# Linear branch's logits beside both value products of a segment, a narrower mask product, a new order of operations

## Chip, core and metric

The kernel runs on one core of one Trainium2 chip. The metric is device time in microseconds (us) of one launch, as the median of several runs. TensorE multiplies matrices into PSUM, which has 8 banks of 128 partitions by 512 fp32 columns; ScalarE and VectorE read PSUM; GpSimd works in SBUF alone. The profile calls the engines PE, ACT, DVE and POOL, and the loading of matmul weights PEld.

## What is computed

Two attention branches over the same 2048 tokens of width 512 are mixed by a gate for each token.

```python
# branch A: a recurrent memory of M=8 tokens, segments of 32 tokens, 32 heads of 128
mask = (idx[:, None] < M) | (idx[:, None] >= idx[None, :])
for s in range(64):
    h = concat([mem, x[32*s : 32*s+32]])            # 40 tokens
    q, k, v = h @ Wq, h @ Wk, h @ Wv                # per head
    p = softmax(where(mask, q @ k.T * 128**-0.5, -1e9))
    o = (p @ v) @ Wo
    mem = o[:8]; outs.append(o[8:])
# branch B: 32 heads of 16, 4 segments of 512 tokens, causal softmax inside a segment,
# plus a linear memory M, z of the segments before, mixed by a gate per head
    p = softmax(q @ k.T * 16**-0.5 + causal_mask)
    a_dot = p @ v
    a_mem = (phi(q) @ M) / (phi(q) @ z + 1e-6)
    o = g * a_mem + (1 - g) * a_dot;  M += phi(k).T @ v;  z += sum(phi(k))
out = gate * a + (1 - gate) * (b @ wo)
```

## The kernel before

**Branch A sets the pace.** Segment s needs the eight memory rows that segment s-1 gives, so 64 segments follow one another. `p_seg` issues one segment. It projects 32 rows, as many as a column group has columns (8 memory rows and 24 tokens), with weights streamed as 128x512 matmuls in four column groups (line 1399), copies PSUM to SBUF (line 999, on ScalarE or VectorE), and transposes q and k by head on VectorE (line 1464). The 32 heads are handled in two halves, r = 0 and 1, of 16 heads. The eight last tokens of each segment are projected four segments at a time (`p_rest`); they are called the rest here, and their queries, keys and values stand in `rem_q`, `rem_k`, `rem_v`.

For each half there are: a mask product H (line 1472) that writes the whole score bank with zeros and large negative numbers, from `neg` and `hide`; the scores S (lines 1479 and 1483) added onto it; an exponential into `PT` (line 1487); the sums over keys by a product U with a block matrix of ones (line 1502); a logarithm and an exponential on ScalarE that give the reciprocals `rc` (lines 1506 and 1508); two multiplications of `PT` by `rc` (line 1510 on VectorE, line 1513 on VectorE or GpSimd); the value product PV (lines 1544 and 1549), whose four row groups write four banks, a *quad*; and two copies of the quad to `OT` (line 999). Behind both halves come the output projection (line 1298, 64 matmuls), a copy `par`, a product `fold` (line 1022, fp32, 16 matmuls) that adds two column groups, and a copy to the next segment's memory rows (line 1321). `PT` holds for each half 224 columns: first 160 (4 heads of 40 queries) against the keys of the 32 rows, then 64 (4 heads of 16 queries) against the keys of the rest. The mask product covers all 224 columns.

**Branch B fills.** It has 16 units (4 segments by 4 groups of 8 heads) of two halves q. A half has four pieces, each of 320 columns of logits: `p_logits` (bL, line 1139, 4 or 8 matmuls in four row groups, into four banks), then `p_exps`: two exponentials of 128x640 on ScalarE (line 1157), a causal mask on GpSimd (line 1163) and, behind the fourth piece, the product with the values (line 1180). From unit 3 on `plan` places these pieces among the segments. `quad` gives each half the segments at which it begins and ends: 17 halves have two segments and 9 have three. A piece in `carry` is issued inside a segment: its logits use columns 160 to 480 of the four banks in which the value product of r=1 writes columns 0 to 160. A piece in `alone` takes four banks of its own. By `plan` 61 pieces are carried and 43 are alone; the 24 pieces of units 0 to 2 are alone as well.

**Tile modes.** TensorE runs three arrangements here: `c32` (four column groups of 32, all large products), `r32` (four row groups of 32 or 16: bL and PV) and `full`. Some products are FLEX: they take `c32` or `full`, whichever the neighbour before has.

**What sets the order.** Each engine runs its list in order. The lists are not found at build time: `ORDER` is a packed string of positions in the list of all operations, engine by engine, in TensorE, ScalarE, VectorE, GpSimd, SyncE order. `sequences` unpacks it; `schedule` then assigns banks along this order, and `waits` derives semaphore waits from the data and bank dependencies. Two engines that read the same PSUM banks are kept apart: the second waits for the first.

Of the kernel before, what the change touches and what calls it, by code (L numbers as in the profile page):

```python
# [8 lines left out]
ALU = mybir.AluOpType  # L9
# [6 lines left out]
    "c-nPZ2S5|&+kf6%lFK3qLs4;|f`D6aQ>!9cC$?gtPPAA@t<+t`g(4MKwQg-4t+wdjja6JI?g1+9i56E~pb!#5a_@cbU6RXP@Ix}Vd+wRPXT9wRxdE(TE7QZ&WVFaSec^ly"  # L16
    "W0(U;D`4TH*ZW(weG>Aa#pLw&KXpC!y~?{dy}d0aZNZOAUtd1a<wTo)(=rQ_mdnh_@jv;t3*XRd$FJ7cS#WkO1e@{#3#w@2nT2&9FI`mtN?1Ki0~6=Z8Ld7VeKZ=D#BSHb"
    "T#3jC+5oE?M4xN_<)rCpuT>VHSzSg?3k@0HK;%g(0svHLbIw9|c4t_1z>KgQmPVYOb}Tot?Xb2@sY?^jM6R{T!)}9bl{>Zng}P7bC}nzp^Fh9W=f1pUq^>vjE2qIya=k3Z"
    "VggW`9~w?B+Yh04PK;Uy5uJ!U;C~K5Yo9}{FAY`L5Jh>}?O?eK5ys+cZDnvKQhlULy#p;=q%go|-Jc_Ut&D=HVzsCuk9tu>DljkGjO#v!!de9u2w4{^Fg^f%vhY|dQrHaS"
    "8Zv*ZE-zNy*H;J4?K;Y<Z|b%(gUUg97|LS~1H>w93fteK+MhF%YX(c(3y6HGLvQ3<o+mI(0{CUJEt8=cq5=@Y*R?GMo1J<Djc*2?gU?Sv%@E>o$4|Ar(8eD?juZ?-bkJ2O"  # L20
    "Z04dsdx=W^^nbAp@71pjuLRQq0G7pmb6Q7PX>IYxDsO7ZA44sQDkrYf!Lk_(U`ocnse&5$08MHgjAkf`Suz*QUO-vOG-ZTR{WM?zK$c)yry0=o7;L)C5Uyz9OqCoys?El7"
    "vu=J`+5CC`+nQs6=o|;>jSis~^G9xoVGi^|UKUk}+`9-gcFInHQkG5b|FuovN|c4d9yh(M423?dSpbFL1Kxpf1;TFv3cW+TX3s!_1wZUbj9>LVz)^%~E7B?|6d%=3gYWyj"
    "tz}-@zmW+R!Hfkba|G(I^IGnx-;z*M$Yub!o%-POUaqK6eXRD%D}5#{c<lNFIALl{RH$LnzVNNM6{!EHrpwE`O1#vm0fV*yj27Hg2jIzzxIzu0d|y{BFV!<<_|G3yO1oLD"
    "-UuxrH#}?&z<7amdT?;)U(JRRoKaeUGVm_anrM&#Y#M9-ZKA+7WsYIpL|#pc%Az)F<#Uo$KLeze0w`(09tD6^so^j{(=x`QD+L0WUnVV?Rkj3va+_22P<ZYa-bAFKRCgq>"
    "iRD3cE@_?x!@ZXF>%nl&=QBZW`pR)D3k}nM<9NQS2djFITj}fbUfnbwm4a4l3cDTlFb!a~z<MIA8?~f+qb$xIZ!0Kl@?s-;-{pjQPxsDnYs;YR3!e(SFOpX){kHEA`O$I!"
    "Hx|=C5<yd@bnEIvUT<U0>KWQ*_^417RC@&>6{WzrDDsTD<)zls63C;fpa&fB+^_+2_HjsEGm~TtL8-A=C7TC3ADKWI4DeDAy)g{hjc5ZY2vLj|m?v&1@h0glE7f&6scwC)"
    "{Z<%qMbKaz#J7)`GJ>$xTC6Pq9t1rsBLz$OmZZzr)g)T4_4`H=9Y+4alg9)6^WjkWcs>n$E6hC(sp*?Fp!=!MVM8++iI+cQLn}}NDRuzIAO}+RT-(R_t4EGSh00*XctZu)"
    "snp~h!)BzUK&lYkQ6#)8yb^ZuN-HYNdRrOE8=XzQaBkw-mmA%L*C~6moAy2=V-$3$j^rU2?G=`YoAQPPoXfvor3Uy;FfRz;esIEOt;uM~=&Rj6$m_X}YBgNlSf-QP>?F_s"
    "`nF8D|J4-Yy7a0113T|Gj%n6^8wr|Msg6W#=g49LHrXaf(5y;O-Xs*w1?E?t#-4=)im}lhZre?CIVhXmkd+#OZ)-Aohdz2uC~62=KLn_+yB5uPf+E!%R2IXJ=?uw)w%6?~"
    "x!Yx+PFn7&361}$Mc$RwCrwh==vMh)DUZCox1V8i>Wzid7EVu_PC%4#d$|zsOIwDu9@AwChYb?%-(ZBAE>fE{9M~GeJ$D8X*3U9WTND-rNuhFDUaI11?r4BN2d@PYEH6M?"  # L30
    "Q**{ZmD-S=tBIHEk%DDL8Y1>R?EO)Y>pgYpn<@k-jKZs!(#bz+NXT>#0?n@)Xg<p>e*ojo2`qmCNc-!?KdA0=#;cfC$xDa_v{XjSuCFy)2Tn~{1~5xdbJ9E5y#44=J_bwX"
    "m`U~$q$ALp#5x}Ckq^BIRyadS6e_yHqy?M&@R#<U<mM59S8e#UZ*9<US;+ZaSE{0I_QydbuYw*l%?~?7DEbJre*?s2C}&s@rLd@!x#8tE8yoTf8p7RB(Aq6<4*GFnIz>n$"
    "Ir=~-Ftt=5E2?t3^(AO?vAQ?u{v>y7q?xNpsZ`!<Oqezo_@DY<fR6eD@uYYo1-V+TT0dG|thH0CVT{`T%T92orBCn7_oO)JXe-g>?@{II)uRfks~?3HubEpyZr^LN=OH9J"
    "8BbdXQ#X9GdThrWhs!8V3!1Lr(DkUX{f-@=1xI?e14lg>dUiT_5H^!`jtE#<!6i~0NcuF+hT3JiQW8)9z=AReE8uz89FjJ@?=VOGHj`3s<g($P-kdk8f~$>@#Jd~vf?_Dz"
    "riBkmzTLsg0F}%{$^mg0Pjm(%k8aOlx@GeT5P2bG-g`Bq&ME<a6Db(i_RcL3U^RFYKzrlCc#`6zbjm-1nx2qeqBiRw@Kv>Eq%puuQGy2@3<B(!40u@4#G_|BlFqr)-8hlq"
    "&qN0|z7P}jWbmkoz5EeC8$oPsfTv&Py>Jz54t1Yh=3qycH-9O#Y`$dsJ?YHBEYne7ffK4>wkCjP<>>NFVYjCWJO=`7+qd(WOSaBV7lDezMP27nebVh+R(S0=$<?1D3Jb-J"
    "3?zPr3VVyI9HD)4lE96Og&(NB!_o4|q@jQC1(3ZnT7gV9{&I`T#S5A0IK{oLs*_tNJ3r3YY07z@=8Y)i3Jg?v^QO@)XmqQkm-VBb8&q_qIx<L~gC2*Xj{CHeJ0CegUR0e!"
    "5b_e6u)H%y-;l%!yF%&)<RoBp_qnC{EExV8qjfk4ieUGT7<K9a6=!lWin@YPWb<obx#17MM*Gs(0Qj@_*zY=YEXl{wV7US9?}V-%55&(kb|jK1Q>O;YsXkz*Wq5=SY+XM="
    "!5GP<1@JT2$_)szY5Xk#uTfo2E5U9dSF{IkBAGaiYbJt44>oA@5NS=bGGlg=;nG27QmV+MM*L%7k*mR$(;dJ!c2{7tJdQ}Fgd+bkjXiyqS1CN<$3Z<IH2Z^11xQ;m_A=Av"
    "nr+d78OzFPo-la{!qK;?Fz>1&eMwa)Qr&AsG$yL_#xJZ)VGH&B;38F{Lh?8QjUTScflBA#Xrfc+k&Bmlasv;iPKEEQYO`mm5!N*!Ls-BIy_yrkJ-RW;)Sjf3j;N=E>x~Ek"  # L40
    "wSFsMDf7n&q~j_w0R$&hlkyAjbCJ;{p-QRW+qyh^&iZ-NX_>a9HOXRQNsnBf#BRCQ8W64p{{0RRvch1_b0#uZ;jiIYw?nj3SNk7}?h~@R(b&sr0Fj7QGCUM+5RmDghHzwd"
# [541 lines left out]
class Kernel:  # L583
# [24 lines left out]
    def alloc(self):  # L608
# [50 lines left out]
        self.hide = t("hide_sb", [128, 224])  # L659
        self.neg = t("neg_sb", [128, 128])  # L660
        self.hT = [t("hT%d" % i, [128, C, 32]) for i in range(2)]

# [64 lines left out]
    def build(self):  # L727
# [23 lines left out]
        for key, u, q, p in self.alone:  # L751
            self.at(key, self.p_piece, u, q, p)
# [857 lines left out]
```

## Time and profile before

| what | value |
|---|---|
| median of 3 runs | 832.67 us (831.51 to 833.88) |
| span of the profiled execution (first to last instruction) | 828.3 us |
| granted TensorE clock | 0.999 |
| TensorE busy | 804.8 us, 97% |
| VectorE busy | 617.3 us, 75% |
| ScalarE busy | 564.1 us, 68% |
| GpSimd busy | 262.3 us, 32% |

The profile gives a span and no device time of its own for the profiled execution; the median of the runs stands 4.4 us above that span. Matmuls overlap (four column groups run side by side), so the mean duration of one matmul is longer than the distance from one start to the next. TensorE's cost is read from those distances or from the chain of waits, which credits each instruction with the time from the end of the one before to its own end. The costliest groups, by line:

```
L1399 PE MATMUL pb<-Wv_sb,hT 128*32 128x512 bf16 x2048 | 162.7, 380 | 0.1
L1298 PE MATMUL pb<-Wo_sb,OT_sb 128*32 128x256 bf16 x4096 | 131.9, 273 | 1.0 <-DVE OT_sb L999 0.4
L1157 ACT ACTIVATE PTB<-pb 128x640 bf16<-128x640 f32 x240 | 158.4, 703 | 35.2 <-PE pb L1139 30.3
L1163 POOL TENSOR_SCALAR_AFFINE_SELECT PTB<-PTB 128x512 bf16<-128x512 bf16 x120 | 77.8, 649 | 105.7 <-ACT PTB L1157 99.2
```

### The profile page before, as it was taken

To read this page: it belongs to the slowest core of one execution; us is meant where nothing else is said; L and a number is where in the kernel's file an instruction comes from. 1 tells how busy PE (TensorE), PEld (TensorE's weight loads), DVE (VectorE), ACT (ScalarE), POOL (GpSimd) and SP (SyncE) were. 2 spreads that over 40 slices of the span, in tenths; PEclk is the share of its full clock that TensorE was granted. 3 is DMA by queue.
4 is the path that set the end of the run, shared out by engine and by line. 5 is a ranking of instruction groups with operands and counts; after the bars stand their busy time and mean duration, and the time that the engine had idled before them with its cause. 6 is when DMAs were issued, how large, how long until landed. Compare 5 with 4: busy or idle time off the path is not lost.

```text
span 828.3 us, 53292 instructions
## 1 busy us (share of the span) xinstructions
PE 804.8 (97%) x24456; PEld 521.1 (63%) x24474; DVE 617.3 (75%) x1398; ACT 564.1 (68%) x1279; POOL 262.3 (32%) x576
## 2 busy tenths in 40 slices
PE   8999999999999999999999999999999999999987
PEld 4445666766666566666767666666666665666654
DVE  4788668769778767778687687776877767876775
ACT  4677766777767666676667766677666677767663
POOL 3552231223323323223233233423223223323340
PEclk9999999999999999999999999999999999999999
DMA  9982111111111111111012111100111110010001
GB/s 344 413 248 58 41 26 39 38 45 31 42 30 30 33 28 43 28 34 46 26 33 53 38 27 31 34 22 11 49 38 39 34 26 8 13 26 21 21 21 36
DMA packets 71701, 45.63 MB, mean 55 GB/s; under 512 B 50046, under 2 KB 69942, under 8 KB 69942
## 3 DMA queue, kind: packets, MB, share of 16 engines
q1 hardware_dynamic: 70422, 41.18, 17.2%
q8 instruction: 192, 3.15, 1.6%
q10 hardware_dynamic: 1056, 1.05, 0.4%
q14 instruction: 31, 0.25, 0.1%
HBM read 30.72 MB, written 8.87 MB: 48 GB/s over the span
## 4 chain that ended last, share of the span: by engine, by line
PE 86%; DVE 4%; ACT 4%; DMA 3%; issue 1%; SPq 1%; POOL 1%; DVEq 0%; POOLq 0%; ACTq 0%
PE pb L1399 47%; PE pb L1298 17%; PE pb L1022 7%; PE pb L1139 3%; PE pb L1544 3%; PE pb L1180 2%; PE pb L1024 2%; DMA st<-in_A_mem_dram 2%; PE pb L1502 2%; PE pb L1479 1%; DMA out_dram<-stg 1%; PE pb L1228 1%; ACT rc_sb L1508 1%; ACT rc_sb L1506 1%; PE pb L1483 1%
## 5 line engine op out<-in xcount | busy, mean ns | idle before, releaser
L999 ACT ACTIVATE st<-pb 128x512 bf16<-128x512 f32 (+2 forms) x313 | 149.1, 494 | 103.5 <-PE pb L1399 78.3
L1157 ACT ACTIVATE PTB<-pb 128x640 bf16<-128x640 f32 x240 | 158.4, 703 | 35.2 <-PE pb L1139 30.3
L1399 PE MATMUL pb<-Wv_sb,hT 128*32 128x512 bf16 x2048 | 162.7, 380 | 0.1
L1399 PE MATMUL pb<-Wq_sb,hT 128*32 128x256 bf16 (+1 forms) x3072 | 139.4, 308 | 0.1
L1399 PE MATMUL pb<-Wk_sb,hT 128*32 128x512 bf16 x2048 | 133.2, 379 | 0.2
L1298 PE MATMUL pb<-Wo_sb,OT_sb 128*32 128x256 bf16 x4096 | 131.9, 273 | 1.0 <-DVE OT_sb L999 0.4
L1513 POOL TENSOR_TENSOR PT_sb<-PT_sb,rc_sb 128x64 bf16<-128x64 bf16 x90 | 33.4, 371 | 248.2 <-ACT rc_sb L1508 239.7
L1163 POOL TENSOR_SCALAR_AFFINE_SELECT PTB<-PTB 128x512 bf16<-128x512 bf16 x120 | 77.8, 649 | 105.7 <-ACT PTB L1157 99.2
L1298 PEld LDWEIGHTS pb<-Wo_sb,OT_sb 128*32 128x32 bf16 x4096 | 100.7, 96 | 15.6 <-ACT OT_sb L999 3.8
L1399 PEld LDWEIGHTS pb<-Wq_sb,hT 128*32 128x32 bf16 x3072 | 83.3, 97 | 39.8 <-issue 1.9
L1464 DVE STREAM_TRANSPOSE QT_sb<-st 128x256 bf16<-128x256 bf16 (+1 forms) x192 | 94.4, 510 | 17.1 <-ACT st L999 15.2
L1464 DVE STREAM_TRANSPOSE KT_sb<-st 128x512 bf16<-128x512 bf16 x128 | 89.4, 700 | 12.2 <-ACT st L999 10.5
L1399 PEld LDWEIGHTS pb<-Wk_sb,hT 128*32 128x32 bf16 x2048 | 57.7, 97 | 43.0 <-issue 1.7
L999 ACT ACTIVATE OT_sb<-pb 128x320 bf16<-128x320 f32 (+1 forms) x140 | 58.2, 428 | 37.7 <-PE pb L1549 36.4
L999 DVE CAST OT_sb<-pb 128x320 bf16<-128x320 f32 (+1 forms) x120 | 56.9, 479 | 31.4 <-PE pb L1549 29.6
L1399 PEld LDWEIGHTS pb<-Wv_sb,hT 128*32 128x32 bf16 x2048 | 52.8, 97 | 17.8 <-DVE ao L1328 0.6
L1506 ACT ACTIVATE rc_sb<-pb 128x160 f32<-128x160 f32 x128 | 38.9, 304 | 35.5 <-PE pb L1502 34.5
L1321 DVE CAST hT<-pb 128x32 bf16<-128x32 f32 x63 | 12.0, 191 | 66.7 <-PE pb L1022 66.5
L1487 ACT ACTIVATE PT_sb<-pb 128x224 bf16<-128x224 f32 x128 | 45.7, 357 | 17.3 <-PE pb L1483 12.6
L999 DVE CAST V_sb<-pb 128x512 bf16<-128x512 f32 x65 | 44.5, 685 | 9.9 <-PE pb L1399 8.9
L1510 DVE TENSOR_TENSOR PT_sb<-PT_sb,rc_sb 128x160 bf16<-128x160 bf16 x128 | 42.7, 333 | 8.1 <-ACT rc_sb L1508 6.8
L999 ACT ACTIVATE stg<-pb 128x512 bf16<-128x512 f32 (+1 forms) x68 | 37.9, 559 | 13.6 <-PE pb L1399 9.6
(204 smaller groups left out, 1468.9 us busy)
## 6 DMA issues: line engine op xcount, KB each, us to landing
Wv_sb<-in_A_Wv_dram SPq DMA_DIRECT2D x4, 1024.0 KB, 11.3
Wk_sb<-in_A_Wk_dram SPq DMA_DIRECT2D x4, 1024.0 KB, 20.2
Wq_sb<-in_A_Wq_dram SPq DMA_DIRECT2D x4, 1024.0 KB, 26.1
Wo_sb<-in_A_Wo_dram SPq DMA_DIRECT2D x4, 1024.0 KB, 21.3
rest_v<-stg SPq DMA_DIRECT2D x112, 32.0 KB
rem_v<-rest_v SPq DMA_DIRECT2D x28, 128.0 KB, 3.1
a_rows<-ao SPq DMA_DIRECT2D x63, 32.0 KB
stg<-a_rows SPq DMA_DIRECT2D x15, 128.0 KB
```

The costliest lines, as they stand in the source:

```text
L999: self.P.op(("act", "dve"), (lambda a: a.activation(dst, src(), ACT.Copy), lambda d: d.tensor_copy(dst, src())), reads=reads, writes=write ...
L1022: ins = pe.matmul(out[32 * c:32 * c + 32], lhsT[:, 32 * c:32 * c + 32], rhs, start=start, stop=stop, tile_position=(0, 32 * c), **kw)
L1139: ins = pe.matmul(pb[slot.banks[i]][:, base + a - lo:base + b - lo], KT[r0:r1, 128 * kc:128 * kc + 128], Q[r0:r1, t0 + a:t0 + b], start=Tr ...
L1157: P.op("act", (lambda dst=dst, src=src: lambda a: a.activation(dst, src(), ACT.Exp, scale=0.25))(), reads=[pair], writes=["%s%d_%d" % (nam ...
L1163: P.op("gp", (lambda pt=pt, ii=ii: (lambda g: g.affine_select(pt, pt, ([[0, len(ii)]] if len(ii) > 1 else []) + [[1, 128]], ALU.is_ge, 0.0 ...
L1298: ins = pe.matmul(pb[so.b][p0:p0 + 32, 0:256], tok(r, g, l), self.Wo[:, h, 256 * d:256 * d + 256], start=(r == 0 and g == 0 and l < 2), st ...
L1399: ins = pe.matmul(self.pb[sl.b][32 * g:32 * g + 32, 0:hi - lo], x[:, c, 0:32], cols, start=(c == 0), stop=(c == C - 1), tile_position=(0, ...
L1464: op("dve", (lambda dst=dst, src=src: lambda d: d.transpose(dst, src))(), reads=["st%d%s" % (i, tag)], writes=["%sT%d%s" % (kind, r, tag)] ...
L1487: op("act", lambda a: a.activation(PT[:, r, :], pb[rb.b][:, 0:224], ACT.Exp, scale=SCALE), reads=[rb], writes=["PT%d" % r, "PT%dr" % r], n ...
L1506: op("act", lambda a: a.activation(rc[:, r, :], pb[rb.b][:, 0:160], ACT.Ln), reads=[rb], writes=[rr], name="ln%d_%d" % (s, r), cost=t_act( ...
L1510: op("dve", lambda d: d.tensor_tensor(PT[:, r, 0:160], PT[:, r, 0:160], rc[:, r, :], ALU.mult), reads=[rp, rr], writes=[rp], name="nrm%d_% ...
L1513: op(("dve", "gp"), tuple((lambda e: e.tensor_tensor(rest, rest, late(rc[:, r, :]), ALU.mult)) for _ in range(2)), reads=[rp + "r", rr], w ...
```

## The change

Three things change together.

1. `plan` has no `alone` list from unit 3 on. A half of two segments puts its four pieces beside (s, r=0), (s, r=1), (s+1, r=0), (s+1, r=1); a half of three segments beside (s, r=1), (s+1, r=0), (s+1, r=1), (s+2, r=1). So 104 pieces are carried, 43 of them by a value product of r=0.
2. Scores and `PT` are laid out by head: 4 heads of 56 columns, of which the first 16 belong to the keys of the rest and the other 40 to the 32 rows. The columns that need a mask are then the first 40 of each 56, so `hide` has 160 columns and the mask product writes 160 of the 224 columns (the scores' matmuls write the rest first). All readers and writers of `PT` take the new pattern.
3. `ORDER` is another string, for all engines.

```diff
-            for p, at in enumerate(((s - 0.3, s, s + 0.7, s + 1), (s, s + 0.7, s + 1, s + 2), (s, s + 1, s + 2, s + 3))[min(end - s, 4) - 2]):
-                if at == int(at):
-                    self.carry[int(at), 1] = (u, q, p)
-                else:
-                    self.alone.append((at, u, q, p))
+            for p, at in enumerate(((0, 1, 2, 3), (1, 2, 3, 5), (1, 3, 5, 7))[min(end - s, 4) - 2]):
+                self.carry[s + at // 2, at % 2] = (u, q, p)
...
-        for key, u, q, p in self.alone:
-            self.at(key, self.p_piece, u, q, p)
...
-        hide = [("hide", self.hide[0:32, lo:hi].rearrange("p (h q) -> p h q", h=4)) for lo, hi in ((0, 160), (160, 224))]
+        hide = self.hide[0:32, :].rearrange("p (h q) -> p h q", h=4)
+        hide = [("hide", hide[:, :, lo:hi]) for lo, hi in ((16, 40), (0, 16))]
...
+        def by_head(t):
+            return t.rearrange("p (l q) -> p l q", l=4)
+
+        mine, rest = [by_head(PT[:, r, :])[:, :, 16:56] for r in range(2)], [by_head(PT[:, r, :])[:, :, 0:16] for r in range(2)]
...
-                return self.mm(pe, m, pb[rb.b][:, 0:224], self.neg[:, :], self.hide[:, :], True, True, skip_group_check=True)
+                return self.mm(pe, m, by_head(pb[rb.b][:, 0:224])[:, :, 0:40], self.neg[:, :], self.hide[:, :].rearrange("p (h q) -> p h q", h=4), True, True, skip_group_check=True)
...
-                        ins = pe.matmul(pb[rb.b][32 * g:32 * g + 32, l * L:(l + 1) * L], KT[:, 16 * r + 4 * g + l, :], QT[:, 16 * r + 4 * g + l, :],
+                        ins = pe.matmul(pb[rb.b][32 * g:32 * g + 32, 56 * l + 16:56 * l + 56], KT[:, 16 * r + 4 * g + l, :], QT[:, 16 * r + 4 * g + l, :],
...
-                    ins = pe.matmul(pb[rb.b][32 * g:32 * g + 32, 160:224], Kr[:, h0:h0 + 4].rearrange("p h k -> p (h k)"), QT[:, h0:h0 + 4, 24:40],
+                    ins = pe.matmul(by_head(pb[rb.b][32 * g:32 * g + 32, 0:224])[:, :, 0:16], Kr[:, h0:h0 + 4].rearrange("p h k -> p (h k)"), QT[:, h0:h0 + 4, 24:40],
...
-                    for k, (dst, src) in enumerate(((o[:, 0:160], PT[:, r, 0:160]), (late(o[:, 0:160]), PT[:, r, 160:224]))):
+                    for k, (dst, src) in enumerate(((by_head(o[:, 0:160]), mine[r]), (late(o[:, 0:160]), rest[r]))):
...
-            op("dve", lambda d: d.tensor_tensor(PT[:, r, 0:160], PT[:, r, 0:160], rc[:, r, :], ALU.mult), reads=[rp, rr],
+            op("dve", lambda d: d.tensor_tensor(mine[r], mine[r], by_head(rc[:, r, :]), ALU.mult), reads=[rp, rr],
...
-                        ins = pe.matmul(o[:, L * l:L * l + L], Vs[p0:p0 + 32, r, 128 * l:128 * l + 128], PT[p0:p0 + 32, r, L * l:L * l + L],
+                        ins = pe.matmul(o[:, L * l:L * l + L], Vs[p0:p0 + 32, r, 128 * l:128 * l + 128], mine[r][p0:p0 + 32, l],
...
-                    ins = pe.matmul(o, Vr[p0:p0 + 32, 128 * r:128 * r + 128], PT[p0:p0 + 32, r, 160:224],
+                    ins = pe.matmul(o, Vr[p0:p0 + 32, 128 * r:128 * r + 128], rest[r][p0:p0 + 32],
```

The multiplication of the rest's part (line 1513) takes the 64 columns `rest[r]` in the same way. `p_seg` itself already issues a carried piece for either r: logits ordered behind the sums U, then PV, the two copies of the quad, then the piece's exponentials and mask.

More of the change, by code (lines that the diff above doesn't have):

```diff
@@ L20 @@
[L20 to L31, printed above, removed]
@@ L705, in plan @@
         self.quad = [int(round(self.pace(self.ALONE + i / 2))) for i in range(n + 1)]
-        self.carry, self.alone = {}, []
+        self.carry = {}
         for i, (s, end) in enumerate(zip(self.quad, self.quad[1:])):
@@ L1471, in f_hide @@
             def f_hide(pe, m):
-                return self.mm(pe, m, pb[rb.b][:, 0:224], self.neg[:, :], self.hide[:, :], True, True, skip_group_check=True)
-            op("pe", f_hide, reads=["neg", "hide", "st%d" % i], writes=[rb], name="H%d_%d" % (s, r), cost=0.1, prio=prio, mode=FLEX)
+                return self.mm(pe, m, by_head(pb[rb.b][:, 0:224])[:, :, 0:40], self.neg[:, :], self.hide[:, :].rearrange("p (h q) -> p h q", h=4), True, True, skip_group_check=True)
+            op("pe", f_hide, reads=["neg", "hide", "st%d" % i], writes=[rb], name="H%d_%d" % (s, r), cost=0.072, prio=prio, mode=FLEX)
             def f_sc(pe):
```

124 lines of the change are left out of this document (66 added, 58 removed).

## Prediction

> **What bounds the kernel now.** I read the busy times first, then the same in stretches, then the chain of waits, and last single groups.
>
> ```profile
> PE 804.8 (97%) x24456; PEld 521.1 (63%) x24474; DVE 617.3 (75%) x1398; ACT 564.1 (68%) x1279; POOL 262.3 (32%) x576
> PE 86%; DVE 4%; ACT 4%; DMA 3%; issue 1%; SPq 1%; POOL 1%; DVEq 0%; POOLq 0%; ACTq 0%
> 200.00:400.00 200.00, 196.31 (x6233) 129.37 (x6226) 152.24 (x345) 139.11 (x321) 59.93 (x131) 1.00 0.14 33
> 400.00:600.00 200.00, 196.46 (x6130) 133.87 (x6130) 151.24 (x346) 140.30 (x321) 64.75 (x139) 1.00 0.14 33
> ```
>
> TensorE is busy 98% of each middle stretch (196.3 and 196.5 of 200 us) at the full clock, VectorE 76%, ScalarE 70%. What TensorE no longer has to do comes off the time, as long as the others keep up. A busy TensorE is not at its peak, though; the chain of waits near 400 us shows what each step costs it:
>
> ```profile
> 399.98 1.75 PE pb L1298 x64
> ...
> 402.16 0.11 PE pb L1022 x16
> 402.27 0.25 PE pb L1139 x4
> 402.52 4.29 PE pb L1399 x79
> ...
> 410.31 0.21 PE pb L1544 x16
> ...
> 411.52 0.25 PE pb L1139 x4
> 411.77 0.10 PE pb L1544 x16
> 411.87 0.04 PE pb L1549 x4
> 411.90 1.86 PE pb L1298 x63
> ...
> 418.82 0.10 PE pb L1022 x4
> ```
>
> At 410.31 the value product PV follows `c32` work and takes 0.21 us; at 411.77 it follows logits of its own mode `r32` and takes 0.10. A change of mode thus costs 0.11 on the way in. On the way out, the output projection (L1298) takes 1.86 for 63 matmuls behind a PV and 1.75 for 64 behind its own kind: 63 of them would be 1.72, so 0.14. At 402.27 stands a lone piece: 0.25 us, entry included, between two `c32` products. At 418.82 the mask product H takes 0.10 in four matmuls.
>
> **What the change removes: mode changes.** A lone piece costs 0.25 plus an exit of 0.11 to 0.14, together 0.36 to 0.39. A carried one costs 0.25 less the 0.11 that its PV then saves: 0.14. So 0.22 to 0.25 is saved for each piece that really stood alone. 43 pieces move; at most that is 86 changes of mode. Not all vanish: I unpacked both order strings into the names of operations and counted neighbours of different mode on TensorE, FLEX products taking their neighbour's: 389 changes before and 327 behind the change, 62 fewer (the new list puts other work between PV of r=0 and of r=1, which stood side by side at times). 62 x 0.11 = **6.8 us**; by the exit's price 62 x 0.14 = 8.7. I take 6.8, from the row where two like instructions differ in the neighbour alone.
>
> **Fewer mask columns.** 64 of 224 columns go, in 128 products of 0.10 us: 0.10 x 64/224 = 0.029 each, 3.7 us. The rows by shape agree within a little: a 128x224 mask matmul lasts 259 ns, a 128x160 one of U 236 ns, so 23 ns less, 2.9 us. Lower bound nothing, if loading weights set the pace of these four. I take **3.5**.
>
> **The new patterns.** The mask product now writes runs of 40 columns with gaps, the scores of the rest write runs of 16. Today's nearest rows: PV's 64 columns of the rest, written in runs of 16, last 184 ns; the scores' 64 contiguous columns last 196 ns.
>
> ```profile
> L1022 PE MATMUL pb<-hide_sb,neg_sb 128*32 128x224 bf16 x504 | 35.5, 259 | 0.0
> L1502 PE MATMUL pb<-PT_sb,ones_sb 128*32 128x160 bf16 x488 | 31.3, 236 | 0.2
> L1483 PE MATMUL pb<-QT_sb,rem_k 128*32 128x64 bf16 x512 | 27.8, 196 | 0.0
> L1549 PE MATMUL pb<-PT_sb,rem_v 32*128 32x64 bf16 x512 | 25.6, 184 | 0.0
> L1513 DVE TENSOR_TENSOR PT_sb<-PT_sb,rc_sb 128x64 bf16<-128x64 bf16 x38 | 9.1, 238 | 2.0 <-ACT rc_sb L1508 1.5
> ```
>
> So gaps cost nothing: 0; the upper bound is the last rival below. The Trainium skill, PSUM — Partial Sum Buffer (Specifications), says that any non-contiguous access pattern slows matmuls significantly; the two rows just named don't agree for runs of 16, and it gives no factor. On VectorE the multiplication of 160 columns takes 333 ns and that of 64, read with gaps from `rc`, 238: 1.0 ns for each further column, gaps or none, so the strided form should stay at 333. For GpSimd (371 ns) there is no strided row; bounds -0.13 (VectorE's 238) and +0.3 (its 128x256 product at 0.63), hidden behind the sums' filler; I take 0.
>
> **What moves and doesn't change.** The same 104 pieces run from unit 3 on: logits, 208 exponentials of 0.70, 104 masks of 0.65 on GpSimd. None of a piece's instructions issues a DMA, and the new string has the same 367 on SyncE, so no transfer passes a queue anew. The string has 29 operations fewer on ScalarE and 44 more on VectorE, 15 fewer on GpSimd. By their rows (a 128x512 copy 0.59 on ScalarE, 0.68 on VectorE; `par` 0.38 and 0.42) ScalarE falls by about 18 us to 66%, VectorE rises by about 25 to 78%. Both stay below TensorE, so this costs nothing by itself.
>
> **What it adds: a wait.** A carried piece's exponentials wait for PV and for both copies of the quad, and the quad's four banks come free only then. The quad of r=1 needs the other four. So in the 43 segments in which both halves carry a piece, PV of r=1 and its logits can't begin before the exponentials of r=0 are done. The timeline shows how long that takes for a quad of today:
>
> ```profile
> 423.44 0.21 PE L1549 MATMUL pb<-PT_sb,rem_v 32*128 32x64 bf16 x4
> 423.71 0.44 ACT L999 ACTIVATE OT_sb<-pb 128x320 bf16<-128x320 f32 x1 [0.84 <-PE pb L1549]
> 424.05 0.70 ACT L1157 ACTIVATE PTB<-pb 128x640 bf16<-128x640 f32 x1
> ```
>
> First exponential at 424.05, a second right behind it would end at about 425.4 (0.7 each, slightly overlapped): 1.8 us from the end of PV at 423.65. With a logarithm or reciprocal of the other half between (0.30 and 0.34) it is 2.1 to 2.4. In the new list the work that TensorE has between PV of r=0 and the logits for r=1, priced by the distances between starts in this trace, has a median of 2.06 us over segments 8 to 61 (0.98 in the old one). So the wait is covered, just; without that cover it is 43 x 2 us. In 17 cases an exponential of r=0 stands ahead of the reciprocal of r=1 on ScalarE; behind it queue `rc`, the multiplications and PV of r=1, and later `par`, which holds `fold` and the next segment. Bounds: nothing, or the 0.3 by which 2.4 exceeds 2.06, 43 times: 13 us. A gain is possible as well: against the lower third of like distances the old list loses some 28 us of TensorE time in small waits, and a list with 43 fewer free-standing quads might lose 5 less. I take **+1.5**, near the covered end, since the median stands above the undisturbed 1.8.
>
> **Sum.** -6.8 - 3.5 + 1.5 = -8.8 on a span of 828.3: 819.5. The 4.4 us that the median stands above the span stay: 823.9, say **824.0**. Pricing the whole of both lists by those distances gives -11.4 without the mask, so the sum is not the deep end.
>
> **Rivals.** *The quads collide.* ScalarE can't finish the exponentials of r=0 in the 2.06 us, PV of r=1 waits 0.3 us in each of 43 segments, and the recurrence takes that up undiminished: -10.3 + 13 = +2.7, 835.4. For it: both quads fill all eight banks, ScalarE is at 70% and its list is strict. Against: ScalarE loses 18 us of copies. It decides from 0.24 us in each segment on (10.3/43). Chance 0.18.
>
> *The saved switches were hidden anyway.* If the supply of instructions to TensorE paces the dense parts (the blocks of 256 instructions arrive 4.06 us apart at the median, 3.28 at the least, and the new list has 72 matmuls more), only the mask's columns or less come off: -3, 829.7. For it: waits named "issue" before PV's weight loads are 13.0 us; against: hardly any reaches a matmul. It also covers a change that doesn't do what it says. Chance 0.11.
>
> *More comes off.* The full price of both lists, 11.4, the mask's 3.5 and 3 us of small waits: -17.9, 814.8. Chance 0.08.
>
> *Gaps cost.* Were each strided column to take twice its time, the mask product's 160 would cost 0.07 more and the rest's 64 scores 0.03, 128 times: +12.8, so +2.5 with the sum without its wait, 835.2. The 184 against 196 ns contradict it. Chance 0.02. The Trainium skill, PSUM — Partial Sum Buffer (Specifications), has this slowing as its rule.
>
> **From these to the numbers.** The forecast has 0.61, with a range of its own of 819 to 828.5. Within 0.3% (2.5 us, about what this measurement can tell) is "same". Faster: 0.59 of the forecast, 0.06 of the hidden switches, 0.08 = 0.73. Slower: 0.15 of the collision and the 0.02 of the gaps = 0.17. Same: what is left of the forecast (0.02), of the hidden switches (0.05) and of the collision (0.03) = 0.10. The range of 8 in 10 runs from 815 to 836, which takes in the collision.
>
> **What would show it.** Right: fewer rows of L1139 in the chain that stand between `c32` products, PV at 0.10 in both halves, mask matmuls of about 236 ns, TensorE still 97% busy, its sum near 795. Wrong: a new wait of TensorE's weight loads at L1139 or L1544 for ACT L1157 of some tenths of a us some 40 times; L1022 or L1502 longer than now; VectorE's L1510 above 333 ns; a longer stretch before the first segment.

## The result, and the profile after

The changed kernel takes **859.16 us** (857.08 to 860.39, 4 runs) against 832.7 for the one before: 1.0309 times as long, 95% interval 1.0286 to 1.0332. It is slower by some 26 us, where 8.7 less were forecast. Below, a step of 0.001 in such a ratio is 0.83 us; the ratios compare kernels better than medians, since each is taken against the kernel before on the same chip.

The page of the changed kernel: busy times, TensorE's busy slices, the granted clock, the chain by engine.

```profile
PE 815.2 (95%) x24535; PEld 508.9 (60%) x24546; DVE 637.0 (74%) x1442; ACT 548.5 (64%) x1249; POOL 252.6 (30%) x561
PE   3999999999999999999999999999999999999987
PEclk7899999999999999999999999999999999999999
PE 82%; DVE 5%; ACT 4%; DMA 4%; SPq 2%; issue 2%; POOL 1%; DVEq 0%; ACTq 0%; POOLq 0%
```

TensorE's sum was forecast near 795 and went up to 815.2 (a matmul at half clock counts longer). Two things are new: the first slice (21 us) has TensorE at three tenths and the clock at seven, and TensorE's share of the chain is 82%, not 86. VectorE rose to 637.0 us (forecast about 642) and ScalarE fell to 548.5 (about 546), as counted from the string.

**The start.** The timeline of ScalarE, VectorE and SP in the changed kernel (start, duration, in brackets the idle time before and who ended it):

```profile
20.47 0.23 ACT L864 ACTIVATE rc_sb<-beta_sb 128x32 f32<-128x32 bf16 x1 [18.40 <-DMA st<-in_gate_w_dram]
...
1.85 0.11 DVE L838 MEMSET neg_sb<- 128x64 uint32 x1
20.73 0.18 DVE L866 TENSOR_SCALAR rc_sb<-rc_sb 128x32 f32<-128x32 f32 x1 [18.77 <-ACT rc_sb L864]
20.95 0.35 DVE L868 RECIPROCAL rc_sb<-rc_sb 128x32 f32<-128x32 f32 x1
21.22 0.69 DVE L916 COPY xT<-pb 128x512 bf16<-128x512 bf16 x2
...
0.79 0.40 SPq L790 DMA_DIRECT2D beta_sb<-in_B_beta_dram  x1
5.20 2.05 SPq L888 DMA_DIRECT2D Wv_sb<-in_A_Wv_dram  x4
7.72 0.26 SPq L792 DMA_DIRECT2D st<-in_gate_w_dram  x1
```

The new lists put the sigmoid of `beta` third on ScalarE and ahead of the copies of `xT` on VectorE. `beta` is loaded first of all, but it shares a semaphore with two other small loads, and the wait is for the group's total; the last of the group is issued behind 4 MB of weights. So ScalarE stands 18.40 us, VectorE 18.77, and the copies that every projection needs begin at 21.22 us (before: 5.36). The Trainium skill, DMA: Bandwidth & Descriptors (Why a DMA increments its semaphore by 16 and not by 1), advises one semaphore for each load in flight, because a part of the count proves nothing; this trace shows the other side, a full count that waits for the slowest member. Segment 0's key projection (its first weight load) began at 45.0 us instead of 30.8.

**The segments.** Busy time of PE, PEld, DVE, ACT and POOL in two middle stretches, then the clock:

```profile
200.00:400.00 200.00, 194.50 (x6126) 124.17 (x6123) 155.48 (x356) 132.75 (x306) 54.64 (x123) 0.99 0.15 34
400.00:600.00 200.00, 195.05 (x6062) 124.79 (x6059) 156.14 (x354) 133.54 (x304) 59.63 (x129) 1.00 0.15 32
```

Fewer matmuls in each 200 us (6126 and 6062; before 6233 and 6130) and TensorE less busy (196.3 and 196.5 before). Waits of TensorE's weight loads: us in total, times, longest us. A weight load can wait while matmuls run, so these sums need not be lost time. Of the changed kernel:

```profile
PEld pb L1132 <- ACT PTB L1150: 11.2, 34, 1.4
PEld pb L1291 <- ACT OT_sb L992: 9.9, 34, 0.5
PEld pb L1500 <- ACT PT_sb L1485: 22.5, 72, 0.5
PEld pb L1015 <- ACT st L992: 15.5, 46, 0.8
```

Before, the logits waited for the exponentials 3.5 us in 11 times, the output projection for `OT` 3.8 in 12, the sums for the scores' exponential 14.2 in 48, the mask product for a copy 8.8 in 24. TensorE's loads wait for ScalarE more often, though ScalarE has less to do.

Pricing every step of both lists by the lower quarter of the distances between starts of like steps with like neighbours, over both traces, gives for segments 3 to 61: before 710.0 us = 681.9 of work + 28.1 of small waits; after 720.6 = 673.3 + 47.3. **By this pricing the work fell by 8.6 us and the waits rose by 19.2.** The growth of 10.6 is measured; its split is an estimate (telling steps apart by shape and count alone gives 4.4 less work and 14.9 more waits). The changes of mode did become fewer: in the traces PV stands right behind logits 103 times (61 before), and neighbouring matmuls change between the row-group form and the others 298 times (372 before). The groups of the new patterns:

```profile
L1015 PE MATMUL pb<-hide_sb,neg_sb 128*32 128x160 bf16 x512 | 31.6, 233 | 0.0
L1508 DVE TENSOR_TENSOR PT_sb<-PT_sb,rc_sb 128x160 bf16<-128x160 bf16 x128 | 43.3, 338 | 9.0 <-ACT rc_sb L1506 7.7
L1481 PE MATMUL pb<-QT_sb,rem_k 128*32 128x64 bf16 x512 | 27.3, 196 | 0.0
```

A mask matmul went from 259 to 233 ns, VectorE's strided product from 333 to 338, the scores written with gaps stayed at 196: the patterns cost nothing.

### The profile page after: what moved, and what is told of

Read it like the earlier page. It is cut to its first block, busy times and chain, and to the rows that moved or that the text cites. A ratio compares the mean times of both kernels' runs of the same rounds, so it can differ in the third digit from the quotient of the medians.

```text
span 855.1 us, 53411 instructions
## 1 busy us (share of the span) xinstructions
PE 815.2 (95%) x24535; PEld 508.9 (60%) x24546; DVE 637.0 (74%) x1442; ACT 548.5 (64%) x1249; POOL 252.6 (30%) x561
## 4 chain that ended last, share of the span: by engine, by line
PE 82%; DVE 5%; ACT 4%; DMA 4%; SPq 2%; issue 2%; POOL 1%; DVEq 0%; ACTq 0%; POOLq 0%
PE pb L1392 44%; PE pb L1291 16%; PE pb L1015 7%; PE pb L1132 3%; PE pb L1541 2%; PE pb L1017 2%; PE pb L1173 2%; PE pb L1500 2%; DMA st<-in_gate_w_dram 1%; PE pb L1477 1%; DMA rest_v<-stg 1%; SPq L1364 1%; DMA rem_v<-rest_v 1%; ACT rc_sb L1506 1%; ACT rc_sb L1504 1%
## 5 line engine op out<-in xcount | busy, mean ns | idle before, releaser
L992 ACT ACTIVATE st<-pb 128x512 bf16<-128x512 f32 (+2 forms) x326 | 154.2, 489 | 148.0 <-PE pb L1392 101.9
L1150 ACT ACTIVATE PTB<-pb 128x640 bf16<-128x640 f32 x240 | 161.4, 703 | 21.0 <-PE pb L1132 15.5
L1392 PE MATMUL pb<-Wv_sb,hT 128*32 128x512 bf16 x2048 | 158.6, 380 | 0.1
L1291 PE MATMUL pb<-Wo_sb,OT_sb 128*32 128x256 bf16 x4096 | 145.8, 275 | 2.0 <-issue 1.0
L1462 DVE STREAM_TRANSPOSE QT_sb<-st 128x256 bf16<-128x256 bf16 (+1 forms) x192 | 94.7, 510 | 10.6 <-ACT st L992 9.0
L1462 DVE STREAM_TRANSPOSE KT_sb<-st 128x512 bf16<-128x512 bf16 x128 | 89.3, 698 | 10.6 <-ACT st L992 8.5
L1510 POOL TENSOR_TENSOR PT_sb<-PT_sb,rc_sb 128x64 bf16<-128x64 bf16 x81 | 29.6, 365 | 212.7 <-ACT rc_sb L1506 211.2
L992 DVE CAST OT_sb<-pb 128x320 bf16<-128x320 f32 (+2 forms) x125 | 59.0, 481 | 31.7 <-PE pb L1546 29.5
L992 ACT ACTIVATE OT_sb<-pb 128x320 bf16<-128x320 f32 (+1 forms) x135 | 55.5, 427 | 40.6 <-PE pb L1546 38.5
L1504 ACT ACTIVATE rc_sb<-pb 128x160 f32<-128x160 f32 x128 | 38.9, 304 | 35.0 <-PE pb L1500 32.9
L992 DVE CAST V_sb<-pb 128x512 bf16<-128x512 f32 x80 | 54.5, 683 | 8.3 <-PE pb L1392 6.4
L1392 PEld LDWEIGHTS pb<-Wv_sb,hT 128*32 128x32 bf16 x2048 | 48.8, 97 | 18.9 <-issue 1.0
L1392 PE MATMUL pb<-Wk_sb,xr 128*32 128x512 bf16 x512 | 43.7, 382 | 1.9 <-DMA rest_v<-stg 1.9
```

What stands on the lines that cost most here:

```text
L992: self.P.op(("act", "dve"), (lambda a: a.activation(dst, src(), ACT.Copy), lambda d: d.tensor_copy(dst, src())), reads=reads, writes=write ...
L1150: P.op("act", (lambda dst=dst, src=src: lambda a: a.activation(dst, src(), ACT.Exp, scale=0.25))(), reads=[pair], writes=["%s%d_%d" % (nam ...
L1291: ins = pe.matmul(pb[so.b][p0:p0 + 32, 0:256], tok(r, g, l), self.Wo[:, h, 256 * d:256 * d + 256], start=(r == 0 and g == 0 and l < 2), st ...
L1392: ins = pe.matmul(self.pb[sl.b][32 * g:32 * g + 32, 0:hi - lo], x[:, c, 0:32], cols, start=(c == 0), stop=(c == C - 1), tile_position=(0, ...
L1462: op("dve", (lambda dst=dst, src=src: lambda d: d.transpose(dst, src))(), reads=["st%d%s" % (i, tag)], writes=["%sT%d%s" % (kind, r, tag)] ...
L1504: op("act", lambda a: a.activation(rc[:, r, :], pb[rb.b][:, 0:160], ACT.Ln), reads=[rb], writes=[rr], name="ln%d_%d" % (s, r), cost=t_act( ...
```

## Experiments

Names beginning with a have the changed plan and order, with b the order before. All ratios are against the kernel before:

| run | median us | ratio | 95% interval |
|---|---|---|---|
| a_beta | 845.15 | 1.0137 | 1.0109 to 1.0165 |
| a_beta_wide | 847.54 | 1.0173 | 1.0147 to 1.0199 |
| a_start | 844.13 | 1.0139 | 1.0099 to 1.0178 |
| a_sp | 839.52 | 1.0083 | 1.0053 to 1.0112 |
| a_spq | 841.22 | 1.0102 | 1.0063 to 1.0141 |
| a_hold | 843.72 | 1.0126 | 1.0091 to 1.0161 |
| a_short | 845.61 | 1.0157 | 1.0123 to 1.0191 |
| a_thin | 837.77 | 1.0075 | 1.0046 to 1.0104 |
| a_none | 844.00 | 1.0133 | 1.0082 to 1.0183 |
| a_lean | 839.88 | 1.0082 | 1.0054 to 1.0110 |
| a_lean_hold | 837.41 | 1.0056 | 1.0037 to 1.0075 |
| a_few | 839.85 | 1.0080 | 1.0051 to 1.0108 |
| b_mask | 831.91 | 0.9983 | 0.9971 to 0.9995 |
| b_short | 830.54 | 0.9973 | 0.9952 to 0.9995 |
| b_thin | 827.28 | 0.9944 | 0.9926 to 0.9962 |
| b_none | 827.66 | 0.9925 | 0.9901 to 0.9948 |
| b_lean | 825.50 | 0.9908 | 0.9874 to 0.9941 |
| b_few | 835.32 | 1.0023 | 1.0009 to 1.0037 |

### The start, and the layout alone

`a_beta` gives one load its own semaphore, nothing else:

```diff
+        self.g_beta = P.group("beta")
-        dma(self.g_small, lambda s: s.dma_start(self.beta[:, :], ...
+        dma(self.g_beta, lambda s: s.dma_start(self.beta[:, :], ...
```

> The changed kernel, with the load of beta counted on a semaphore of its own in place of the one it shares with the gate weights and the first memory. Start theory: in the new VectorE list the first step on beta stands ahead of the four copies of x, and its wait (18.8 us in the changed kernel's trace) is for all three small loads, two of which are queued behind 4 MB of weights; segment 0's first projection began 14.2 us later than before. Then this run gives those 14 back: 843 to 847 us. Rival: the start is late because of the new order of the loads themselves; then 855 us or more.

The ratio fell from 1.0309 to 1.0137, 14.3 us: **the start is more than half of the loss.** `b_mask` takes the other end: the plan and the string of before, with the new layout and the mask of 160 columns.

> The kernel before, its own order and its own lone pieces, with only the new layout of the scores and the mask product over 160 columns. The term of the sum holds: mask products fall from 96 to 69 ns between starts, 128 times, so 829.2 us (828 to 830.5). Rival, gaps in the patterns cost: no gain or slower, 833 or more. Rival, the saved time turns into waits in front of the scores: 832 to 833.

0.9983: 1.4 us off, where 3.5 were forecast. That misses its range of 828 to 830.5 and lies nearest to the last rival, by which the saved time turns into waits. It is the one version without left-out work that is faster than both kernels. `a_beta_wide` is `a_beta` with the old layout and 224 columns:

> The run a_beta with the old layout, so the mask product covers 224 columns again. If TensorE's own work still sets the time of the changed kernel, it is 3.4 us slower than a_beta. If the recurrence sets it and TensorE waits, the 27 ns more in each mask product come out of those waits: 0 to 1 us slower than a_beta.

3.0 us slower than `a_beta` (intervals just overlapping). So the layout is worth 1.4 us in the old order and 3.0 in the changed one, where 3.5 were forecast, and the loss is not its doing.

### The rest of the start, and SP's queue

`a_start` moves three things in `a_beta`'s lists: on SP the loads of x first; on ScalarE and VectorE the sigmoid behind the first exponentials and the copies of `xT`.

```diff
-SP: beta wBv x x x x wBq Wv Wv Wv Wv mem0 gate_w ...
+SP: x x x x beta wBq wBv Wv Wv Wv Wv gate_w mem0 ...
-ScalarE: tables wBk sigmoid(beta) bE ...       VectorE: ... sigmoid(beta) xT xT ...
+ScalarE: wBk tables bE bE sigmoid(beta) ...    VectorE: ... xT xT xT xT bK bQ sigmoid(beta) ...
```

> The changed kernel with beta's load in a group of its own, and with the start put back in three places: SP issues the four loads of x first, as the kernel before does, beta's load behind them; ScalarE and VectorE do the sigmoid of beta behind the first exponentials and behind the copies of xT, not ahead of them. All later work stays in the changed order. With beta's group alone the first transposes began at 9.07 us (before: 4.93), TensorE stood idle for 2.53 us and the granted clock was 0.5 for 3.41 us after it; segment 0's first projection came 2.1 us later than before, segment 2's 4.8. Theory A (the rest of the loss is mostly of the start): 5 to 7 us off the 845.15 of beta's group alone, 838 to 840, since the lag at segment 5 was 6.2 us. Theory B (most of what is left is lost in the segments): 1 to 3 us off, 842 to 844, and the lag against before still grows by 8 us or more from segment 5 to the end.

No gain (1.0139 for 1.0137), although segment 0's key projection came 2.8 us earlier than in `a_beta` (30.0 us against 32.9). That is less than theory B allowed, and far from A: most of what is left is lost in the segments. The trace of `a_beta` shows one such place, in segment 14 (timeline of PE and SP; stretches with busy times of the five engines and the clock):

```profile
239.33 0.62 PE L1393 MATMUL pb<-Wk_sb,xr 128*32 128x512 bf16 x4 [1.53 <-DMA rest_v<-stg]
239.73 3.33 PE L1292 MATMUL pb<-Wo_sb,OT_sb 128*32 128x256 bf16 x64
...
230.26 0.53 SPq L1365 DMA_DIRECT2D rest_v<-stg  x1
230.84 1.22 SPq L905 DMA_TRANSPOSE xT<-in_A_x_dram  x1
232.09 1.44 SPq L1411 DMA_DIRECT2D rem_v<-rest_v  x1
233.58 0.56 SPq L1573 DMA_DIRECT2D a_rows<-ao  x1
234.18 0.52 SPq L1365 DMA_DIRECT2D rest_v<-stg  x1
...
235.80:239.20 3.40, 1.70 (x76) 1.17 (x72) 2.22 (x6) 2.63 (x8) 1.79 (x4) 1.00 0.34 78
239.20:242.60 3.40, 3.27 (x60) 2.28 (x64) 0.00 (x0) 0.29 (x1) 0.64 (x1) 0.50 0.02 5
```

Between the four stores of one group of rest rows stand other transfers, so the group's buffer comes free late; TensorE waits 1.53 us and then runs at half clock: the 64 matmuls of the output projection take 3.33 us instead of about 1.8. Counting the unpacked lists, nothing stands between the stores of a group before; in the changed list 107 other issues do. `a_sp` is `a_start` with the four stores of each group side by side on SP:

```diff
-SP: store0 x rem_v a_rows store1 a_rows store2 wqB store3
+SP: store0 store1 store2 store3 x rem_v a_rows a_rows wqB
```

> The changed kernel with the start put back as in the run before (beta's group, x first, the sigmoid later), and with one more thing put back: on SP the four stores of a group of rest rows stand together again. In the order before nothing stands between the four stores of a group; in the changed order 107 other issues stand there (transposed loads of x at 1.2 us of the queue's time, loads of rem_v at 1.4, stores of a_rows at 0.5), and TensorE waits for these stores 3.1 us in 4 places, 1.5 of them in segment 14 with the granted clock at 0.5 for 3.41 us behind it. Theory SP (the new order of SP's queue is a main cause of what is left): 4 us or more off the 844.13, 840 or less, and no half clock at 236 to 240 us. Rival: the waits in the segments come from the chain of the recurrence and take up what is saved here: 0 to 3 us off, 841 to 844.

1.0083, 4.7 us off `a_start` (the intervals overlap a little, so the size is uncertain), and the place is mended: the four stores stand as one row, and the clock from 236 to 242 us is 1.00.

```profile
230.10 2.20 SPq L1363 DMA_DIRECT2D rest_v<-stg  x4
```

`a_spq` puts the rest of SP's queue back as far as it goes.

> The run with start and stores put back (839.52), with SP's whole queue after the start put back as far as it goes: of the issues whose data are ready, SP takes the one that stands first in the order before. In the changed order the transposed loads of x and the loads of the linear branch's weights stand tens of issues from where the order before has them, and TensorE still waits 1.5 us for rem_v in the run with the stores together. Theory SP (what is left, 7.6 us above the old order with the new layout, is still its queue's): 4 us or more off, 835 or less. Rival (what is left lies in the order of the four compute engines, whose chain is longer): 0 to 3 us off, 836.5 to 840.

No further gain (1.0102). It is no clean step beyond `a_sp`, since 19 issues stand between stores of a group again; against `a_start` it is 3.1 us faster. With nearly all of SP's queue in its old order the time stays, so the remaining 8.3 us between `a_sp` and `b_mask` are not found there.

### The held banks and the moved pieces

`a_hold` and `a_short` change the exponentials of the 43 pieces of r=0 in `a_beta`, at unchanged lists:

```diff
-  ... [:, :, base:base + n]                 # the piece's banks
+  ... self.W["k"][:, 0:2, 0:n]              # a_hold, for r == 0
+  ... [:, :, base:base + 16]                # a_short, for r == 0
```

> The kernel with beta's group alone, in which the exponentials of the 43 pieces that ride in the first value product (r=0) read a tile of weights in SBUF in place of their banks: the logits of these pieces are computed and not used, the exponentials run at the same places of ScalarE's list over as many columns, and the four banks come free as soon as the product's own two copies are done. Theory quads (banks held until the exponentials are done make the second half of the segment wait: the waits of logits for the exponentials grew from 3.5 to 11.2 us, those of the output projection's operand for ScalarE from 3.8 to 9.9): 6 to 12 us off, 833 to 839. Rival ScalarE (the 1.4 us of exponentials stand in ScalarE's list between the two halves of a segment, whoever holds the banks): within 2 us of 845.15. Rival list (the new order has other work at worse places, and the banks have no part in it): within 2 us as well; the short exponentials of the next run tell these two apart.

> The kernel with beta's group alone, in which the two exponentials of each of the 43 pieces of the first value product (r=0) take 16 columns of a bank in place of 320 (the other columns keep what they held): about 0.5 us less of ScalarE for each, some 45 us less over the kernel, at the same places of the list, and banks that come free that much earlier. Theory quads: 6 to 14 us off, 831 to 839, as with the exponentials from SBUF or a little more. Rival ScalarE: 8 to 16 us off, 829 to 837, where the run with exponentials from SBUF gains nothing. Rival list: 1 to 4 us off, no more than the same cut gains in the old order (next run).

1.0126 and 1.0157 against 1.0137: nothing outside the intervals. Theory quads and the rival ScalarE, which asked for 6 us or more, did not come true, though the 86 short exponentials took 194 ns each in place of 703, some 44 us of ScalarE's work. Yet the wait that was to show the held banks did go away; first two lines of `a_hold`, then of `a_short`:

```profile
PEld pb L1133 <- ACT PTB L1151: 1.4, 4, 0.4
PEld pb L1133 <- issue: 11.6, 45, 0.4
```

```profile
PEld pb L1133 <- ACT PTB L1156: 3.5, 4, 1.4
PEld pb L1133 <- issue: 12.4, 46, 0.4
```

It was 11.2 us in 34 times in `a_beta`. Another wait stands in its place: the same loads wait for nothing that the profile shows ("issue") 11.6 us in 45 times and 12.4 in 46, against 4.7 in 18 in `a_beta`. What ends that wait isn't shown. `b_short`, the same cut in the old order, tells how little these exponentials weigh there:

> The same cut in the old order: the kernel before with the new layout and the mask of 160 columns (831.91), in which the exponentials of the same 43 pieces, which there have banks of their own and stand in the segment's tail, take 16 columns in place of 320. Quads and ScalarE: 0 to 4 us off, 828 to 832, since these exponentials stand outside the stretch from the first value product to the second. List: as much off as in the changed order, within 2 us. If it takes off 8 us or more, ScalarE's time counts wherever it stands, and the two orders don't differ by it.

0.9973, 0.8 us off `b_mask`. To take the pieces' logits away as well, `a_none` and `b_none` reduced them to four matmuls of 16 columns:

> The changed kernel with start and stores put back (839.52), in which the 43 pieces of the first value product have almost no work: their logits are four matmuls of 16 columns in place of 4 or 8 of up to 320, their exponentials take 16 columns in place of 320. It leaves that part of the linear branch out. Theory pieces (these pieces stand in the chain of the segments, with their logits ahead of the first value product and their exponentials ahead of its copies): 5 us or more off, 834.5 or less, and at least 4 us more than the same cut takes off in the order before. Rival (they fit beside the segment's own work; what is left over is the order of the rest): 0 to 3 us off.

> The same cut in the order before (new layout, mask of 160 columns; 831.91), where the same 43 pieces have banks of their own. Both theories: 0 to 4 us off, 828 to 832; the cut of their exponentials alone took 1.4 us off.

`a_none` became 4.2 us slower than `a_sp` with less to do (their intervals overlap), `b_none` 4.8 faster than `b_mask`. Neither theory had `a_none` slower, and why it was isn't shown. In the next section a changed number of TensorE's instructions alone moves the time of one order; `a_thin` and `b_thin` therefore make the cut at an unchanged number (every matmul of these logits 16 columns wide).

```diff
+        if self.brief(u, q, p):                                              # the 43 pieces
+            parts = [(kc, a, a + 16) for kc, a, b in parts if a < b][:1]     # a_none, b_none
+            parts = [(kc, a, a + 16) for kc, a, b in parts if a < b]         # a_thin, b_thin
```

> The changed kernel with start and stores put back (839.52), in which the 43 pieces of the first value product are thin and TensorE has as many instructions as without the cut: each matmul of their logits takes 16 columns, and each of their exponentials 16 in place of 320. It leaves that part of the linear branch out. The run with fewer instructions became slower by 4.5 us, and so did the old order when 1152 instructions were taken out (835.32 against 825.50, with 13 us of waits for nothing the profile shows, at multiples of 256 of TensorE's loads and matmuls), so this one keeps their number. Theory pieces (the pieces stand in the chain of the segments): 5 us or more off, 834.5 or less. Rival (what is left is the order of the rest): 0 to 3 us off, 836.5 to 840.

> The same in the order before (831.91 uncut; 827.66 with its instructions cut as well, 830.54 with the exponentials alone). Both theories: 0 to 4 us off.

0.7 us off `a_sp`, 3.2 off `b_mask`. Theory pieces is refuted: the moved pieces are no heavier in the changed order than in the old one, and the rival "order of the rest" stands.

### How much TensorE's work is worth

`a_lean` (from `a_sp`) and `b_lean` (from `b_mask`) narrow three of four quarters of rk and rq to 64 columns:

```diff
+                h = lo + 64 if name[0] == "r" and kind != "v" and c0 else hi
-                        cols = part[:, g] if kind == "v" else part[:, g, lo // 32:hi // 32]
+                        cols = part[:, g] if kind == "v" else part[:, g, lo // 32:h // 32]
```

> The kernel of the run before this one (start and stores put back) with less work to fill the segments: of the projections of rest rows onto keys and queries (rk, rq), three of the four quarters take 64 columns in place of 512, so 192 quarters of 0.216 us become about 0.06 (an estimate, from the 64-column rows of the logits), some 30 us less of TensorE. It leaves that part of the projection out. What TensorE then does not need shows how long the chain of the segments itself is. Theory chain (sharing makes the chain of a segment longer: 2.3 us from the first value product to the second, against 1.5): falls by 8 to 18 us, and by at least 8 less than the order before under the same cut. Rival filler (the chain is no longer than before, other work only stands at worse places): falls by as much as the order before, or more, so that the two come within 8 us of each other.

> The same cut of rk and rq in the order before (new layout, mask of 160 columns; 831.91 uncut). It leaves the same part out. Both theories: 18 to 28 us off, 804 to 814. If it falls by under 10, the chain sets the time in the old order too, and the cut of TensorE's work by the change could not have been worth what was forecast.

The median distance from a quarter's start to the next step fell from 216 ns to 29 to 38, 192 times: some 35 us of work. **It was worth 6.2 us in the old order and nothing (0.1) in the changed one.** Theory chain asked for a fall of 8 or more in the changed order, the rival for as much as in the old one; neither came true as put. For the old order the sign named ahead did, a fall by under 10: the chain of the segments sets much of the time there too. The pages of `b_lean`, then `a_lean`:

```profile
PE 780.7 (95%) x24456; PEld 508.4 (62%) x24474; DVE 615.3 (75%) x1398; ACT 562.2 (68%) x1279; POOL 260.5 (32%) x576
PE 75%; ACT 8%; DVE 8%; issue 3%; DMA 2%; POOL 2%; SPq 1%; DVEq 0%; POOLq 0%; ACTq 0%
```

```profile
PE 788.8 (94%) x24535; PEld 498.5 (60%) x24546; DVE 637.7 (76%) x1442; ACT 547.4 (66%) x1249; POOL 253.1 (30%) x561
PE 76%; ACT 9%; DVE 7%; issue 3%; DMA 2%; POOL 1%; SPq 1%; DVEq 0%; POOLq 0%; ACTq 0%
```

TensorE's share of the chain fell from 87 and 84% to 75 and 76%, and ScalarE and VectorE took its place. I read this so: right beneath TensorE's work lies the segment's chain across the engines. The two orders stand 14.5 us apart when lean, 8.3 when not, so the changed one's chain is the longer. `a_lean_hold` frees the banks there too, by the edit of `a_hold`:

> The lean kernel in the changed order, with the exponentials of the 43 pieces of the first value product reading SBUF, so that nothing but the product's own copies holds the four banks. If the held banks lengthen the chain: 6 us or more below the lean kernel with shared banks. If they do not (the second product waits for its own softmax, or for the place it has in TensorE's list): within 2 us of it.

2.2 us off `a_lean`, with overlapping intervals: held banks are at most a small part.

A second reading was open, that TensorE is held by the supply of its instructions, which the lean kernels left as many. `a_few` and `b_few` keep one of four row groups of the narrow quarters:

```diff
-                    for g in range(4):
+                    for g in range(4 if h == hi or hi - lo < 512 else 1):
```

> The lean kernel in the changed order, in which the 192 narrow quarters of rk and rq have one row group in place of four: 576 matmuls and as many loads of weights fewer, while TensorE's busy time hardly changes (the quarters are already down to 0.03 us). It leaves that part of the projection out as well. In the traces any 512 records of TensorE (loads and matmuls) take at least 6.3 us and any 1024 at least 14.2, in the order before, the changed one and the lean one alike. Theory issue (TensorE is held by how fast its instructions come, and the lean kernel did not get faster since it had as many): 5 to 16 us below the lean kernel, 824 to 835, since 1152 instructions fewer are worth 16 us at 14.2 us for 1024. Theory chain (the chain of the segments across the engines sets the time): within 2 us of 839.88.

> The same cut of instructions in the order before, against its lean kernel (825.50). Theory issue: 5 to 16 us off, 809 to 820. Theory chain: within 2 us.

Theory issue came true in neither: `a_few` didn't move, as theory chain has it, and `b_few`, against both theories, became 9.6 us **slower** than `b_lean`. TensorE's waits for nothing that the profile shows, `b_lean` first, then `b_few`, and one of them in its timeline:

```profile
PE pb L1023 <- issue: 3.0, 4, 1.0
```

```profile
PE pb L1023 <- issue: 7.5, 9, 1.6
PE pb L1299 <- issue: 4.7, 7, 1.2
...
427.35 0.24 PE L1023 MATMUL pb<-fold_sb,st 128*32 128x16 f32 x5
429.22 0.27 PE L1023 MATMUL pb<-fold_sb,st 128*32 128x16 f32 x10 [1.63 <-issue]
```

`fold` has 16 matmuls and stops for 1.63 us behind the fifth: no data dependency does that. Counting TensorE's loads and matmuls from the start of the trace, this stop and the next four stand at 24074, 24840, 25596, 26358 and 27120: 756 to 766 apart, three times 256 less the few instructions that leave no such record. The trace also shows what ends them. One DMA queue brings instructions in packets of 16 KB, 192 in `b_lean` and 188 in `b_few`, about one for each 256 of TensorE's. Each of the 17 stops longer than 0.25 us in `b_few` ends 1.22 to 1.52 us after such a packet has landed; the one before this restart landed at 427.84. So late instructions stop TensorE at single places; whether they also slow dense stretches by less isn't shown. The stops sum to 3.9 us in `b_mask`, 7.2 in `b_lean` and 13.4 in `b_few`, which is 6.2 of the 9.6 us. They grew most, from 4.3 to 12.2 us, at lines 1023 and 1299, with `fold` and the output projection, for which the next segment waits. They don't make the difference between the orders: they sum to 6.4 us in `a_sp`, but to 4.4 in `a_thin` against 5.5 in `b_thin`, and these two stand 10.9 us apart.

## Why the prediction was wrong, step by step

**Work of TensorE: right in kind, its size near.** Fewer mode changes and mask columns were to take off 10.3 us; the work priced from starts fell by 8.6 (4.4 by the coarser rule), the mask row as forecast.

**"What TensorE no longer has to do comes off the time": this step failed.** 98% busy was read as the bound. 35 us of work taken out brought 6.2 us in the old order; at that rate, an estimate, 10.3 would have been worth 1.8, had nothing else changed. The layout alone brought 1.4. The rate need not hold for all work: what was taken out fills the segments, while the mask product stands in each segment's own chain, and in the changed order its 3.4 us cost 3.0 in `a_beta_wide`. No run takes out the mode changes alone. The rival of the hidden switches (829.7) had that half right, by another cause.

**"No transfer passes a queue anew": this step failed.** The 367 issues on SP were counted and their places not compared. Their order and the sigmoid's place, with a semaphore that three loads share, cost 14.3 us at the start (not in the sum at all; it stood only among the signs of being wrong) and some 4.7 at the stores.

**The wait for the quads, +1.5 in the sum: the named wait came, but the term was too small and stood for the wrong thing; this step failed too.** The wait grew from 3.5 to 11.2 us as its sign said, but taking it away gave 0.9 us in `a_hold` (inside the interval). The rival of colliding quads came out on the right side for a wrong reason. Priced at +1.5, the term should have been for the whole new order of the compute engines: 8.3 us between `a_sp` and `b_mask`. The distances from `fold` to `fold` locate it:

| mean us of a segment | before | b_mask | a_sp | a_thin |
|---|---|---|---|---|
| 42 segments where both halves carry | 12.02 | 12.05 | 12.40 | 12.33 |
| 18 where only r=1 carries | 12.09 | 12.11 | 11.61 | 11.66 |
| first to second value product, the 42 | 1.48 | 1.49 | 2.66 | 2.64 |

42 x 0.35 - 18 x 0.50 = +5.7 us from `b_mask` to `a_sp`, in segments 2 to 61. The rest lies ahead of them, at the 43rd segment with two pieces, segment 1: segment 0's `fold` came 1.9 us earlier, but from there to segment 1's it took 19.75 us instead of 15.21, with TensorE busy for 18.2 of them instead of 15.2 and one stop of 1.55 behind a late packet of instructions. 5.7 - 1.9 + 4.5 is the 8.3. The second value product comes 1.2 us later behind the first where r=0 carries a piece, and stays there when the pieces are thin (2.64) and when the banks are free (2.63 in `a_hold`). So neither the banks nor the pieces hold it; its place in the lists is what is left, as the prediction counted 2.06 us of TensorE's work between the two, 0.98 in the old list.

**The patterns: right**, no cost. **Copies moved from ScalarE to VectorE: counted right.** That this alone costs nothing wasn't tested.

**What stays open:** which of the four compute engines' lists makes the 42 segments longer. Between 80 and 800 us the waits of TensorE's loads and matmuls that ScalarE ends grew most, from 43.8 us in `b_mask` to 70.4 in `a_sp` (those that VectorE ends from 31.5 to 36.6); that points to ScalarE's list and does not show it. A list that issues the second value product earlier, or the old list with the 43 pieces moved, was not tried.

The account, by ratios: 25.7 us lost = 14.3 start - 0.2 from `a_beta` to `a_start` + 4.7 SP's stores + 8.3 left of the new order - 1.4 layout. These are steps along one row of runs, so the sum closes by itself. The 14.3 is clear of the noise, the 4.7 barely, and the 8.3 is what is left over, located and not explained.

## What to carry to other kernels

Where a change brings a new order, compare the whole of it, DMA queue and start included, and not only the neighbours of the edit: some 19 of the 25.7 us lay in queues and start-up that the change was not about. Before a sum of saved work is believed, leave a known amount of that work out and see what it brings: behind an engine that is 97% busy the next bound can stand very near. A wait that grows in the profile is a cause only if the time falls when it is taken away.

## What was not expected of the hardware

- In segment 14 of `a_beta` the granted clock was 0.50 for the 3.4 us behind a stretch of 3.4 us in which TensorE was busy for 1.70, its longest idle time 1.53. At the start of the changed kernel it was 0.50 from 10.2 to 27.3 us, behind a stretch of 3.4 us with TensorE busy for 1.16. The Trainium skill, TensorE: Matmul & The Clock Gate (Part 1: The HAM clock gate), gives the length of that window, and half rate after an idle one. The length agrees; here half a window of idling was enough.
- TensorE stops at multiples of 256 of its instructions, by up to 1.63 us and in the middle of a product, and goes on 1.22 to 1.52 us after a packet of 16 KB of its instructions has landed (17 stops in `b_few`). 1152 fewer instructions cost 9.6 us in one order and nothing in the other.
